# Ordering the opening and the convolution of an S4 + gated-MLP kernel by a list of units

## The chip, the cores and the metric

The kernel runs on one core of a Trainium2 chip. A core has five engines that run their own instruction streams in order and wait for each other through semaphores: PE (TensorE, matmuls; its weight loads are shown apart as PEld), DVE (VectorE), ACT (ScalarE), POOL (GpSimd) and SP (SyncE, which here only issues DMAs). SP, ACT and POOL can each issue DMAs from a queue of their own. The metric is the device time of one execution in microseconds (us). Two times of one kernel are compared by runs of both on the same chip.

## What is computed

The input x has 2048 rows of 576 channels. One modulation vector c gives six rows of 576 through `w_mod`. The first block is a normalised, modulated long convolution; its kernel K (576 channels, 2048 taps) comes from 128 complex poles per channel. The second is a gated MLP. Cut to what matters:

```python
mod = (silu(c) @ w_mod)                     # sa, ca, ga, sb, cb, gb
h = layernorm(x) * (1 + ca) + sa
logdA = dt * (A_re + 1j*A_im);  dB = dt * (B_re + 1j*B_im)
P = exp(logdA[:, :, None] * arange(L))      # 576 x 128 x 2048, complex
K = einsum("dn,dnl,dn->dl", C, P, dB).real
y = irfft(rfft(h) * rfft(K))[:L] + h * Dskip # causal convolution
x = x + ga * y
h = layernorm(x) * (1 + cb) + sb
z = gelu(h @ w_in);  z1, z2 = halves of z
g = w_sp @ layernorm(z2) + b_sp
x = x + gb * ((z1 * g) @ w_out)
```

## The kernel before

**Stages.** `ssm` does the modulation, the first norm, the convolution kernel and the convolution; `Mlp.phase_a` and `phase_b` do the gated MLP, some 1350 us of the span, and are not touched. All of the change is in `ssm`, in what I call the opening (to the first ticks of the loop) and the convolution loop.

**Poles.** `poles(c0, c1, ...)` is a generator: it issues the loads of the seven pole arrays on SP, and each `next` of it then emits a further piece of elementwise work on DVE and ACT. `split3` splits a result into three bf16 parts and writes them to DRAM (`pa_d`, `pb_d`) from POOL's queue. `p0` handles the first chunk of channels (tiles 144 wide, kept in one tile named `et`), `p1` the other three at once (432 wide, tiles `t_n_...`). `poles_load(c)` brings a chunk's parts back as matmul operands `lb`, `lc`, `la`.

**Kernel units.** The kernel's 36 groups of 16 channels each pass through: `e_unit` (three matmuls of `lb` with the table `sel`, then two exponentials on ACT, 1024 and 512 wide, into `et`), `t_unit` (phase matmuls of `lc`, `la` with `sel`, rounding on DVE, or by an ACT pass `ft<-ps` and DVE from group 10 on), `s_unit` (cosine and sine on ACT), `p_unit` (products on DVE into `pg`, `et`), `kg_unit` (32 small matmuls, a copy `kab`), `d_unit` (Dskip), `k1_unit` (matmuls, copy into the `k1` tile of eight groups). Exponential and sine need different ACT tables; each change of table is one ACT_TABLE_LOAD.

**Modulation and norm.** `mod_load(k)` loads one of the six weight blocks in two halves (tiles `wm`, or borrowed `k` tiles for k = 0, 1); `mod_unit(k)` multiplies it by silu(c) and spreads the row over the partitions. The rows 2, 1, 0 give `gar`, `cga`, `sga`/`gsp`, which the first norm needs; 3, 4, 5 are for the MLP. `ln_load(i)` loads four of the 16 row blocks of x into one of two tiles `ln_x`; `ln_stats(i)` computes their mean and deviation; `ln_rows(b)` scales block b on DVE; `ln_pair(b)` does blocks b and b+1: matmuls against the first Fourier stage, in two halves of 288 channels, each copied to `st1o` by ACT and written to `u1_d` in DRAM from POOL's queue.

**Convolution units.** `u_load`/`u_unit` bring back and transform the input, `z_unit` multiplies it by the kernel's transform, `v_unit` goes back one stage and writes `v_d`, `y_load`/`y_unit` the last stage. `u_load` reads rows of all 16 blocks, so it needs every `ln_pair`.

**What sets the order.** The program is written unit by unit. A framework then orders instructions on each engine by a cost model of its own; those issued through `mlp.tied.<engine>` are kept in program order among themselves (they all show line 152, the helper's line, in the profile). V and T (DVE and PE) are `tied` at first and become free later. After a written opening, a loop over 40 ticks runs `p_unit` of tick-2, `t_unit` of tick, `s_unit` of tick-1, `kg_unit` and `d_unit` of tick-3, `k1_unit` of tick-4 and every third tick three `e_unit`s, in one fixed order below tick 10 and another from it. In ticks 0 to 7 the loop also holds one whole `ln_pair`, and the rest of p1 and of the modulation.

Of the kernel before, what the change touches and what calls it, by code (L numbers as in the profile page):

```python
# [9 lines left out]
F32 = mybir.dt.float32  # L10
# [3 lines left out]
AF = mybir.ActivationFunctionType  # L14
# [150 lines left out]
def ssm(tc, I, x1_d, consts_s, dram, mod_d, mlp):  # L165
    nc = tc.nc
    V, A, G, T, S = nc.vector, nc.scalar, nc.gpsimd, nc.tensor, nc.sync
    magic, halfpi, one = consts_s[:, 0:1], consts_s[:, 1:2], consts_s[:, 2:3]
    HC = 288
    CW = 16 * 9 * 128  # L170
    with ExitStack() as ctx:
# [3 lines left out]
        early = ctx.enter_context(ExitStack())  # L175

        u1_d = dram.tile([4, 16, 2, 32, D], F32, name="u1_d")
# [4 lines left out]
        def ps2():  # L182
            return psp.tile([128, 2, 512], F32, name="ps")
# [5 lines left out]
        small = cp.tile([128, 6, 128], F32, name="small")  # L189
# [3 lines left out]
        tb = tabs.enter_context(tc.tile_pool(name="tb", reuse_waits="tile", bufs=2))  # L193
# [141 lines left out]

        gar = ep.tile([128, D], F32, name="gar", bufs=1)
        cga = ep.tile([128, D], F32, name="cga", bufs=1)
# [37 lines left out]
        x4s = {}  # L375
        r1t = {}

        def ln_load(i):
            x4s[i] = ep.tile([128, 4, D], F32, name="ln_x")
            S.dma_start(x4s[i], I["x"][:, 4 * i:4 * i + 4])  # L380

        def r1_load(i):
            r1t[i] = ep.tile([128, 2, 2, 32], F32, name="r1t"), ep.tile([128, 2, 2, 32], BF, name="cs")
            S.dma_start(r1t[i][0], I["c_r1t"][:, 2 * i:2 * i + 2])
            S.dma_start(r1t[i][1], I["c_cs"][:, 2 * i:2 * i + 2])

        lns = {}

# [25 lines left out]
        def ln_rows(b):  # L414
            i, j = divmod(b, 4)
            nm, r = lns[i]
            n = x4s[i][:, j]
            V.scalar_tensor_tensor(n, n, nm[:, j:j + 1], cga, op0=ALU.add, op1=ALU.mult)
            rt = ep.tile([128, 64], F32, name="rt", bufs=4)
            V.tensor_scalar(rt, r1t[b // 2][0][:, b % 2].rearrange("p r k -> p (r k)"), r[:, j:j + 1], None, op0=ALU.mult)  # L420
            return n, rt, r1t[b // 2][1][:, b % 2].rearrange("p r k -> p (r k)")

        def ln_pair(b):
            pair = [ln_rows(b), ln_rows(b + 1)]
            for h in range(2):
                c = slice(HC * h, HC * h + HC)
                o = ep.tile([128, 4, HC], F32, name="st1o")
                pms = [ps2(), ps2()]
                for t, (n, rt, cs) in enumerate(pair):
                    for x, y, st in ((cs, gsp, True), (rt, n, False)):  # L430
                        for g in range(4):
                            rows = slice(32 * g, 32 * g + 32)
                            T.matmul(pms[g // 2][64 * t:64 * t + 64, g % 2, :HC], x[rows], y[rows, c], start=st, stop=not st, skip_group_check=True)
                for k, pm in enumerate(pms):
                    A.activation(o[:, 2 * k:2 * k + 2], pm[:, :, :HC], AF.Copy)
                G.dma_start(u1_d[:, b:b + 2, :, :, c].rearrange("g b r k d -> (b r k) g d"), o)


        k1t = {}
# [229 lines left out]
                at(ty, y_load, c, r)  # L669
                at(ty + 1, y_unit, c, r)  # L670

        p0 = poles(0, 1, mlp.tied.gpsimd, tb.tile([128, 1536], F32, name="et", bufs=5))
        S.dma_start(cT, I["c"])
        mod_load(2)
        ln_load(0)
        S.dma_start(sel, I["c_sel"])
        mod_load(1)
        S.dma_start(small, I["c_small"][:, 128:].rearrange("p (i c) -> p i c", i=6))
        p1 = poles(1, 4, mlp.tied.gpsimd)
        mod_load(0)  # L680
        r1_load(0)
        ln_load(1)
        S.dma_start(msk, I["c_msk"])
        S.dma_start(dsk, I["dsk"])
        r1_load(1)
        V, T = mlp.tied.vector, mlp.tied.tensor
        for _ in range(3):
            next(p0)
        mod_init()
        for _ in p0:  # L690
            pass
# [7 lines left out]
        next(p1)  # L699
        V = nc.vector  # L700
        ln_stats(1)
        sb = cs = None
        for tick in range(NG + 4):
            if tick == 9:
                early.close()
                cs = ctx.enter_context(tc.tile_pool(name="cs", reuse_waits="tile", bufs=1, side="right"))
                sb = ctx.enter_context(tc.tile_pool(name="sb", reuse_waits="tile", bufs=2, side="right"))
                wpre = ctx.enter_context(tc.tile_pool(name="wpre", reuse_waits="tile", bufs=2, side="right"))
            if 9 <= tick < 13:
# [12 lines left out]

            def lag(fn, n):
                if 0 <= tick - n < NG:
                    fn(tick - n)

            if tick == 0:
                for g in range(3):
                    e_unit(g)
            go(y_load)  # L730
            go(u_load)
            es = iter(range(tick, tick + 3) if tick % 3 == 0 and 0 < tick < NG else ())

            def e_one():
                for g in es:
                    e_unit(g)
                    break

            if tick < 10:
                go(z_unit)  # L740
                lag(p_unit, 2)
                lag(t_unit, 0)
                lag(s_unit, 1)
                go(v_unit)
                lag(kg_unit, 3)
                go(u_unit)
                lag(k1_unit, 4)
                go(y_unit)
                lag(d_unit, 3)
                if tick == 0:  # L750
                    T = nc.tensor
                for _ in range(3):
                    e_one()
            else:
                go(z_unit)
                lag(p_unit, 2)
                lag(t_unit, 0)
                lag(s_unit, 1)
                lag(kg_unit, 3)
                lag(k1_unit, 4)  # L760
                go(y_unit)
                go(v_unit)
                e_one()
                go(u_unit)
                lag(d_unit, 3)
                e_one()
                e_one()
            if tick < 5:
                next(p1, None)
                next(p1, None)  # L770
            if tick == 0:
                mod_load(3)
            if 3 <= tick < 6:
                mod_unit(tick)
                if tick < 5:
                    mod_load(tick + 1)
            j = tick
            if j < 8:
                if j in (2, 4):
                    ln_stats(j // 2 + 1)  # L780
                ln_pair(2 * j)
                if j < 6:
                    r1_load(j + 2)
                if j in (1, 3):
                    ln_load(j // 2 + 2)
            if tick in (3, 13, 21):
                poles_load(1 + tick // 10, mlp.tied.gpsimd)


        tabs.close()  # L790
        mlp.nc = mlp.tied
# [1428 lines left out]
```

## Time and profile before

| what | us |
|---|---|
| median of three runs (lowest to highest) | 1770.71 (1767.39 to 1773.47) |
| the profiled execution's own time | 1773.18 |
| its span, first to last instruction | 1771.4 |
| busy in the span: PE, DVE, ACT, POOL | 1666.3, 1259.8, 831.7, 244.1 |
| span up to the end of the convolution stage (about) | 420 |

The profile is one execution. A row of a timeline gives start, duration, engine, line, operation, tiles and count; in square brackets stand the idle time of the engine just before it and what ended that. A row of the DMA list gives the tiles, the issuing queue, the count, the size of one and the median us from issue to landing. Busy time on PE is modelled from pipelined matmuls and is not PE at its peak.

### The profile page before, as it was taken

Reading aid. Unit: us, or ns where it says so; the run is one execution under the profiler, and the core shown is the slowest. Engines: PE = TensorE matmul, PEld = TensorE weight load, DVE = VectorE, ACT = ScalarE, POOL = GpSimd, SP = SyncE. Lnnn points to the kernel's source line nnn. Section 1 sums busy time; section 2 is a strip of 40 time slices with the busy share of each in tenths; the row PEclk is TensorE's granted clock in tenths of the full one; section 3 lists DMA queues with packets and bytes.
Section 4 is the critical chain, followed back from the end, with each engine's and each line's share of the span. In section 5 each row is a group of like instructions: output and inputs, shape, how many; then the busy total and the mean of one; then the engine's idle time right before and its main releaser. Section 6 shows DMA issues by size and latency. Waiting matters only on the chain.

```text
span 1771.4 us, 36409 instructions
## 1 busy us (share of the span) xinstructions
PE 1666.3 (94%) x15174; PEld 1244.5 (70%) x15174; DVE 1259.8 (71%) x2259; ACT 831.7 (47%) x1118; POOL 244.1 (14%) x400
## 2 busy tenths in 40 slices
PE   3687999997899999999999999999999999999999
PEld 1244555565455445787878888888888888888887
DVE  6876999866998997788898767788334477334432
ACT  4758998844577666455434443333232223122210
POOL 3331232233122211000000000000111100111100
PEclk9578999998999999999999999999999999999999
DMA  9466545689598889777665886773766573556531
GB/s 253 139 198 216 162 124 168 198 231 306 179 281 254 244 234 265 267 276 246 222 214 175 306 299 236 255 248 124 251 226 223 195 229 98 195 203 216 188 112 41
DMA packets 183381, 376.24 MB, mean 212 GB/s; under 512 B 39360, under 2 KB 103488, under 8 KB 182448
## 3 DMA queue, kind: packets, MB, share of 16 engines
q1 hardware_dynamic: 140416, 175.23, 32.8%
q0 software_dynamic: 36896, 172.01, 29.6%
q10 hardware_dynamic: 5904, 26.67, 3.7%
q8 instruction: 119, 1.95, 0.5%
q14 instruction: 46, 0.38, 0.1%
HBM read 263.11 MB, written 101.31 MB: 206 GB/s over the span
## 4 chain that ended last, share of the span: by engine, by line
PE 62%; DVE 16%; issue 7%; DMA 6%; ACT 5%; POOL 2%; SPq 1%; ACTq 0%; POOLq 0%; DVEq 0%
PE ps L152 54%; DVE bsz L152 2%; DVE n L152 1%; PE pk L530 1%; DVE zset L152 1%; PE pk L513 1%; DVE gt L152 1%; DVE rq L152 1%; DMA ln_x<-in_x 1%; DMA zset<-set_d 1%; PE pk L592 1%; DVE wso L152 1%; DMA wst<-in_w_in 1%; DMA k<-in_w_mod 1%; PE pk L600 1%
## 5 line engine op out<-in xcount | busy, mean ns | idle before, releaser
L152 PEld LDWEIGHTS <-zset 128*128 128x128 f16 x7182 | 701.9, 98 | 93.0 <-DVE zset L152 8.9
L152 PE MATMUL ps<-wsp,zset 128*128 128x256 f16 x6048 | 667.5, 273 | 7.7 <-DVE zset L152 6.9
L152 PE MATMUL pz<-wz,nt 128*128 128x512 f16 (+1 forms) x1120 | 223.8, 360 | 10.4 <-ACT nt L152 3.8
L152 ACT ACTIVATE z<-gt 128x1024 f16<-128x1024 f32 x56 | 59.0, 1054 | 287.7 <-DVE gt L152 287.7
L152 PEld LDWEIGHTS <-nt 128*128 128x128 f16 x1120 | 109.5, 99 | 118.7 <-issue 5.4
L152 DVE SCALAR_TENSOR_TENSOR gt<-ps,sc,bsp 128x512 f32<-128x512 f32 x36 | 27.0, 750 | 204.7 <-PE ps L152 203.0
L1928 POOL DMA_DIRECT2D zset<-set_d x96 | 50.8, 529 | 869.6 <-PE ps L152 614.3
L152 PE MATMUL ps<-wout,z 128*128 128x288 f16 x1344 | 170.0, 286 | 0.0
L152 PEld LDWEIGHTS <-z 128*128 128x128 f16 x1344 | 131.5, 98 | 33.0
L152 PE MATMUL ps<-n2o,zset 128*128 128x256 f16 x1134 | 128.2, 273 | 0.0
L152 DVE TENSOR_TENSOR raw<-raw 128x512 f32<-128x512 f32 (+2 forms) x228 | 119.1, 528 | 12.1 <-DMA raw<-z_d 7.8
L152 DVE SCALAR_TENSOR_TENSOR gt<-ps,sc,gt 128x512 f32<-128x512 f32 (+1 forms) x180 | 122.2, 696 | 7.6
L152 DVE TENSOR_TENSOR zset<-raw,zset 128x1792 f16<-128x1792 f32 x48 | 96.9, 2019 | 16.4 <-ACT zset L152 16.4
L152 ACT ACTIVATE zset<-raw 128x1792 f16<-128x1792 f32 x48 | 81.0, 1691 | 56.8 <-PE ps L152 23.1
L152 DVE TENSOR_TENSOR z<-ps,z 128x512 f32<-128x512 f32 (+1 forms) x126 | 72.0, 599 | 36.8 <-ACT z L152 25.0
L152 ACT ACTIVATE wsp<-raw,sc 128x1792 f16<-128x1792 f32 x25 | 44.6, 1784 | 42.7 <-DVE raw L152 35.0
L152 ACT ACTIVATE z<-z,sc 128x1024 f32<-128x1024 f32 x21 | 24.1, 1148 | 75.9 <-DVE z L152 71.9
L152 ACT ACTIVATE z<-pz,sc 128x512 f32<-128x512 f32 (+1 forms) x96 | 51.8, 581 | 14.1 <-DMA z_d<-z 7.9
L152 ACT ACTIVATE z<-z,nm,r 128x1152 f32<-128x1152 f32 x24 | 31.5, 1342 | 52.6 <-DVE nm L152 31.9
L152 PE MATMUL ps<-n2q,wf 128*128 128x512 f16 x252 | 55.7, 379 | 0.0
L152 PE MATMUL ps<-wout,z1b 128*128 128x288 f16 x384 | 52.6, 286 | 0.5 <-ACT z1b L152 0.5
L501 DVE TENSOR_TENSOR pg<-et,ft 128x1024 f32<-128x1024 f32 x36 | 43.8, 1217 | 11.5 <-ACT ft L489 11.4
(357 smaller groups left out, 2462.6 us busy)
## 6 DMA issues: line engine op xcount, KB each, us to landing
zset<-set_d POOLq DMA_DIRECT2D x96, 896.0 KB, 5.0
raw<-z_d SPq DMA_DIRECT2D x48, 512.0 KB, 5.6
set_d<-zset ACTq DMA_DIRECT2D x24, 896.0 KB, 6.0
z_d<-z POOLq DMA_DIRECT2D x32, 576.0 KB, 9.7
zset<-wa_d POOLq DMA_DIRECT2D x18, 896.0 KB, 4.9
raw<-in_w_spT SPq DMA_DIRECT2D x25, 512.0 KB, 4.3
set_d<-zset SPq DMA_DIRECT2D x12, 896.0 KB, 5.5
u_d<-st1o POOLq DMA_DIRECT2D x16, 576.0 KB, 4.6
```

The source lines that it names most:

```text
L152: return self.tc.keep_in_program_order(f(*a, **k))
L501: V.tensor_tensor(pr, pi, c3[:, :, None, :].to_broadcast([128, 16, 2, 32]), op=ALU.mult)
L513: T.matmul(pm[32 * j:32 * j + 32, 64 * i:64 * i + 64], x_[:, c], y_[:, c].rearrange("p s j -> p (s j)"), start=st, stop=not st, skip_group ...
L530: T.matmul(pm[64 * ri:64 * ri + 64, 128 * i:128 * i + 128], kk[:, i], r1[ri], start=True, stop=True, skip_group_check=True)
L592: T.matmul(pm[:, w * j:w * j + w], cst[k // 8][:, k % 8], k1t[c][:, k, :w], start=True, stop=True)
L600: T.matmul(pm, inva, zz[:, 0], start=True, stop=False)
L1928: self.nc.gpsimd.dma_start(o, self.set_d[f, j - 1] if j else self.wa_d[f])
```

## The change

The written opening and the ticks 0 to 8 of the loop become one string of tokens, which `early_steps` walks: a letter names the unit, a digit its group, a trailing `g` or `a` puts a load on GpSimd's or ACT's queue instead of SP's. `0` and `#` start p0 and p1, `O` and `P` are one `next` of them, `Q` is `poles_load`, `w` `mod_load`, `M` `mod_unit`, `x` `ln_load`, `S` `ln_stats`, `R` the two `ln_rows` of a pair, `A` and `B` the two halves of `ln_pair` (now `ln_half`), `V` and `T` free the engine. From tick 9 on, three strings give the order of the units by tick modulo 3; exponent groups are drawn singly, two in one tick, one in the next, none in the third. No unit's arithmetic changes.

```diff
-        def mod_load(k):
+        def mod_load(k, q):
...
-                S.dma_start(wmt[k][hh], I["w_mod"][:, k, hh])
+                q.dma_start(wmt[k][hh], I["w_mod"][:, k, hh])
...
-        def ln_pair(b):
-            pair = [ln_rows(b), ln_rows(b + 1)]
-            for h in range(2):
...
+        def ln_half(b, pair, h):
...
-        poles_load(0, mlp.tied.gpsimd)
-        mod_unit(2)
-        ln_stats(0)
-        next(p1)
-        next(p1)
-        mod_unit(1)
-        mod_unit(0)
...
-            if tick < 10:
-                go(z_unit)
-                lag(p_unit, 2)
-                lag(t_unit, 0)
-                lag(s_unit, 1)
-                go(v_unit)
-                lag(kg_unit, 3)
...
-                ln_pair(2 * j)
...
+        early_steps("0 m O O O T c r0g O O r1g l I x0 w2g O O O O M2 O # b a O Q0 e0 V w1g e1 P P t0 P e2 w0g s0 x1g S0 "
+                 "t1 P P s1 p0 M1 M0 P S1 P t2 t3 k0 P s2 p1 R0 A0 B0 e3 R1 e4 r2 d0 w3 e5 s3 k1 p2 A1 B1 t4 x2g R2 P "
...
+        exps = iter(range(9, NG))
+        lagged = {"t": (t_unit, 0), "s": (s_unit, 1), "p": (p_unit, 2), "k": (kg_unit, 3), "d": (d_unit, 3), "1": (k1_unit, 4)}
+        passed = {"z": z_unit, "v": v_unit, "u": u_unit, "y": y_unit}
+        for tick in range(9, NG + 4):
...
+            for n in ('kpt1svyzdeeu', 'ktespy1dzvu', 'ktvsdzuyp1')[tick % 3]:
+                if n == "e":
+                    for g in exps:
+                        e_unit(g)
+                        break
...
```

Three places of the built programs show what moves. The first is the start of PE's stream; `ps<-...,ec` is a modulation product (`wm` is block 2, the two `k_` tiles blocks 1 and 0), `lb` an exponent's operand. Before:

```order
L152 MATMUL ps<-wm,ec 32x288 x12
L152 MATMUL ps<-mpart,small 128x288 x2
L152 MATMUL ps<-k_122,ec 32x288 x12
L152 MATMUL ps<-mpart,small 128x288 x2
L152 MATMUL ps<-k_140,ec 32x288 x12
L152 MATMUL ps<-mpart,small 128x288 x2
L152 LDWEIGHTS lb
L152 MATMUL ps<-sel,lb 128x512
```

and of the change:

```order
L349 MATMUL ps<-wm,ec 32x288 x12
L354 MATMUL ps<-mpart,small 128x288 x2
L448 LDWEIGHTS lb
L448 MATMUL ps<-sel,lb 128x512
...
L349 MATMUL ps<-k_276,ec 32x288 x12
L354 MATMUL ps<-mpart,small 128x288 x2
L349 MATMUL ps<-k_340,ec 32x288 x12
```

The products of blocks 1 and 0 moved behind the first three exponent units and the phase units 0 and 1, which stand at the line of dots.

The second is POOL's stream, which holds its DMA issues. Before:

```order
L152 DMA pb_d<-pt 64x3x144 x2
L152 DMA pa_d<-pt 64x3x144 x4
L152 DMA pb_d<-pt 64x3x144 x2
L152 DMA pa_d<-pt 64x3x144 x2
L152 MEMSET lb 32x1152
L152 DMA lb<-pb_d 48x1152 x2
L152 DMA lc<-pa_d 48x1152 x2
L152 DMA la<-pa_d 48x1152 x2
```

and of the change:

```order
L152 DMA wm<-in_w_mod 96x1728 x2
L152 DMA pa_d<-pt 64x3x144 x2
L152 DMA pb_d<-pt 64x3x144 x2
L152 DMA pa_d<-pt 64x3x144 x2
L152 MEMSET lb 32x1152
L152 DMA lb<-pb_d 48x1152 x2
L152 DMA lc<-pa_d 48x1152 x2
L152 DMA la<-pa_d 48x1152 x2
L152 DMA k_276<-in_w_mod 96x1728 x2
L152 DMA k_340<-in_w_mod 96x1728 x2
L152 DMA ln_x<-in_x 128x2304
```

Block 2 of the weights came in between the pole writes, blocks 1 and 0 and the second x block behind the operands of the first exponents; all four were on SP's queue.

The third is DVE's stream within the poles of the first chunk (144 wide), after its logarithm. Before:

```order
L152 TENSOR_TENSOR t_sq_212<-t_tau_160,pt 128x144
L152 TENSOR_TENSOR t_sq_214<-t_lw,pt 128x144
L152 TENSOR_TENSOR pt<-t_sq_212,pt 128x144
L152 TENSOR_TENSOR pt<-t_sq_214,pt 128x144
L152 TENSOR_SCALAR t_ph<-t_ph 128x144
L152 TENSOR_TENSOR et<-et 128x144
```

and of the change:

```order
L152 TENSOR_TENSOR t_sq_188<-t_tau_120,pt 128x144
L238 TENSOR_TENSOR t_n_A_im<-t_dt,t_n_A_im 128x432
L152 TENSOR_TENSOR t_sq_190<-t_lw,pt 128x144
L152 TENSOR_TENSOR pt<-t_sq_188,pt 128x144
L239 TENSOR_SCALAR t_n_A_im<-t_n_A_im 128x432
L243 TENSOR_TENSOR t_n_A_re<-t_dt,t_n_A_re 128x432
L152 TENSOR_TENSOR pt<-t_sq_190,pt 128x144
L152 TENSOR_SCALAR t_ph<-t_ph 128x144
L152 TENSOR_TENSOR et<-et 128x144
L240 TENSOR_SCALAR t_n_A_im<-t_n_A_im 128x432
L152 TENSOR_SCALAR et<-t_ph 128x144
L247 TENSOR_TENSOR t_q_289<-t_n_C_im,t_n_B_im 128x432
```

The 432-wide steps of the other poles, which stood behind all of the first chunk's, now stand between its steps, the one that reads `t_n_B_im` among them.

More of the change, by code (lines that the diff above doesn't have):

```diff
@@ L421, in ln_rows @@
             return n, rt, r1t[b // 2][1][:, b % 2].rearrange("p r k -> p (r k)")
-        def ln_pair(b):
-            pair = [ln_rows(b), ln_rows(b + 1)]
-            for h in range(2):
[L426 to L436, printed above, removed]
+        def ln_half(b, pair, h):
+            c = slice(HC * h, HC * h + HC)
+            o = ep.tile([128, 4, HC], F32, name="st1o")
+            pms = [ps2(), ps2()]
+            for t, (n, rt, cs) in enumerate(pair):
+                for x, y, st in ((cs, gsp, True), (rt, n, False)):
+                    for g in range(4):
+                        rows = slice(32 * g, 32 * g + 32)
+                        T.matmul(pms[g // 2][64 * t:64 * t + 64, g % 2, :HC], x[rows], y[rows, c], start=st, stop=not st, skip_group_check=True)
+            for k, pm in enumerate(pms):
+                A.activation(o[:, 2 * k:2 * k + 2], pm[:, :, :HC], AF.Copy)
+            G.dma_start(u1_d[:, b:b + 2, :, :, c].rearrange("g b r k d -> (b r k) g d"), o)
         k1t = {}
@@ L670, in ssm @@
                 at(ty + 1, y_unit, c, r)
[L672 to L684, printed above, removed]
@@ L685, in ssm @@
-        r1_load(1)
-        V, T = mlp.tied.vector, mlp.tied.tensor
[L687 to L691, printed above, removed]
-        poles_load(0, mlp.tied.gpsimd)
-        mod_unit(2)
-        ln_stats(0)
-        next(p1)
-        next(p1)
-        mod_unit(1)
-        mod_unit(0)
[L699 to L709, printed above, removed]
+        p1 = p0 = None
@@ L725, in lag @@
                     fn(tick - n)
-            if tick == 0:
-                for g in range(3):
-                    e_unit(g)
             go(y_load)
             go(u_load)
[L732 to L737, printed above, removed]
-            if tick < 10:
-                go(z_unit)
-                lag(p_unit, 2)
-                lag(t_unit, 0)
-                lag(s_unit, 1)
-                go(v_unit)
-                lag(kg_unit, 3)
[L746 to L780, printed above, removed]
-                ln_pair(2 * j)
[L782 to L786, printed above, removed]
+            for n in ('kpt1svyzdeeu', 'ktespy1dzvu', 'ktvsdzuyp1')[tick % 3]:
[3 more added lines that the diff above has]
+                        break
+                elif n in lagged:
+                    lag(*lagged[n])
+                else:
+                    go(passed[n])
+            if tick in (13, 21):
                 poles_load(1 + tick // 10, mlp.tied.gpsimd)
```

65 lines of the change are left out of this document (60 added, 5 removed), and 2 rows, old and new, of the table T.

## The prediction

> **What bounds the kernel now.** The first view read is the busy time by stage. I cut the span where the program changes character: at the first exponential (47.67 us), at the first phase unit of the steady loop (168.78 us), where the last exponentials begin (342.48 us), and at the start of the gated MLP (420 us). Columns: span; busy us of PE, PE weight loads, DVE, ACT, POOL; granted TensorE clock, DMA share, GB/s.
>
> ```profile
> 0.00:47.67 47.67, 19.94 (x87) 7.51 (x87) 27.42 (x91) 21.39 (x45) 17.96 (x33) 1.00 0.97 252
> 47.67:168.78 121.11, 93.62 (x1252) 47.08 (x1251) 91.84 (x192) 88.89 (x133) 29.67 (x45) 0.70 0.56 171
> 168.78:342.48 173.70, 159.32 (x2400) 100.02 (x2400) 160.18 (x200) 159.32 (x213) 49.12 (x85) 0.99 0.58 168
> 342.48:420.00 77.52, 74.95 (x764) 48.79 (x764) 47.86 (x71) 43.51 (x61) 28.96 (x49) 1.00 0.90 255
> 420.00:1771.40 1351.40, 1318.47 (x10676) 1041.14 (x10676) 932.50 (x1708) 518.62 (x670) 118.40 (x190) 0.99 0.66 218
> ```
>
> The change reaches the first four rows; the fifth follows the fourth and only shifts. The lead (first row) is full of DMA (0.97). In the loop (third row) PE, DVE and ACT are all 92% busy: little is left. In the middle (second row) none is above some 77%, though it does the same kinds of unit. That is the room: 121.11 us in which DVE works 91.84. At the loop's 92% the same work would take 100 us.
>
> The second view is the timeline of the lead, engine by engine.
>
> ```profile
> 8.13 0.43 SPq L231 DMA_DIRECT2D t_n_log_dt<-in_A_log_dt  x1
> 15.98 5.58 SPq L231 DMA_DIRECT2D t_n_C_re<-in_A_C_re  x1
> 25.28 0.69 SPq L231 DMA_DIRECT2D t_n_B_im<-in_A_B_im  x1
> 20.13 0.31 DVE L152 TENSOR_TENSOR pt<-t_sq,pt 128x144 bf16<-128x144 f32 x1 [0.39 <-ACT pt L220]
> 34.02 0.61 DVE L152 TENSOR_TENSOR t_q<-t_n_C_im,t_n_B_im 128x432 f32<-128x432 f32 x1 [2.64 <-DMA t_n_B_im<-in_A_B_im]
> 25.38 1.03 POOL L152 DMA_DIRECT2D lb<-pb_d  x2 [1.90 <-DMA pb_d<-pt]
> lb<-pb_d POOLq DMA_DIRECT2D x2, 108.0 KB, 6.6
> la<-pa_d POOLq DMA_DIRECT2D x2, 108.0 KB, 12.2
> 41.85 2.14 PE L152 MATMUL ps<-k,ec 96*32 96x288 f32 x12 [1.34 <-DMA k<-in_w_mod]
> 44.80 2.29 PE L152 MATMUL ps<-mpart,small 128*128 128x288 f32 x4 [0.81 <-ACT mpart L351]
> 47.67 1.02 ACT L451 ACTIVATE et<-ps 128x1024 f32<-128x1024 f32 x1 [2.93 <-PE ps L152]
> ```
>
> The first poles end on DVE at 20.4; their operand lb is fetched at 25.38 and lands 6.6 us later, at 32 to 33. But the exponent's matmul is pinned on PE behind the modulation products, whose last weights come at 41.85, so it runs at 47.0: some 14 us of waiting that it has no need of. The other poles (432 wide) wait too: their last input, B_im, is put to use at 34.02, after SP's queue had stood 5.58 us on one issue.
>
> **The lead, costed.** The sizes of what the queues carry:
>
> ```profile
> k<-in_w_mod SPq DMA_DIRECT2D x4, 648.0 KB, 14.8
> ln_x<-in_x SPq DMA_DIRECT2D x4, 1152.0 KB, 9.4
> sel<-in_c_sel SPq DMA_DIRECT2D x1, 518.0 KB, 12.1
> small<-in_c_small SPq DMA_DIRECT2D x1, 384.0 KB, 17.7
> t_n_B_im<-in_A_B_im SPq DMA_DIRECT2D x1, 216.0 KB, 8.7
> et<-in_A_B_im SPq DMA_DIRECT2D x1, 72.0 KB, 2.2
> 54.98 2.85 DVE L152 RECIPROCAL t_rnd<-t_n_B_re 128x432 f32<-128x432 f32 x1
> ```
>
> Now SP carries ahead of the last pole input: the first chunk 0.50 MB (seven of 72 KB), small 0.38, sel 0.52, x 1.15, the poles 1.51 (seven of 216); sum 4.1 MB, where it carried two modulation weights of 1.30 MB (two halves each) more. GpSimd adds w2 (1.30 MB) beside it. At the row's 252 GB/s, 4.1 MB take 16 us and 5.4 MB 21 us; with the first microseconds, in which little moves, I take B_im at 23 us, 10 us earlier than 33.4.
>
> This has a price. DVE's order now puts large pole instructions between those of the first chunk, the product that reads B_im among them, and DVE runs in order. So the first chunk no longer ends at 20.4: after 23 us some 12 small steps at 0.31 us, ten large at about 0.5 and two round trips to ACT remain, about 10 us, end 33. Then pa_d goes out (two issues, 1.25), lb is cleared (1.05) and fetched. In before, lb and la took 6.6 and 12.2 us in a full DMA stage; now the queues are nearly empty at 35 us (w3 alone runs before it), and I take 4. First exponential near 40 to 41 instead of 47.67: **7 us** gained. Bounds: 0 (B_im as late as before, p0's end at 43) to 12 (no wait in p0's steps).
>
> w1, w0 and the second x block follow la on GpSimd, issued near 39 us: 2.59 MB at 252 GB/s is 10.3 us, so M0's product runs at 50 to 52 instead of 41.85 to 47. The norm's first matmul needs it through sga and gsp:
>
> ```profile
> 55.91 0.47 PE L433 MATMUL ps<-gsp,cs 32*64 32x288 bf16 x4 [0.74 <-ACT et L451]
> 154.92 0.47 PE L433 MATMUL ps<-gsp,cs 32*64 32x288 bf16 x6 [0.77 <-ACT st1o L435]
> 57.76 1.22 DVE L479 COPY ft<-ps 128x1024 f32<-128x1024 f32 x1
> 108.05 1.82 SPq L380 DMA_DIRECT2D ln_x<-in_x  x1
> 116.44 1.18 DVE L408 BATCH_NORM_STATS2 bs<-ln_x 128x6 f32<-128x288 f32 x3 [4.85 <-DMA ln_x<-in_x]
> 128.83 1.15 ACT L489 ACTIVATE ft<-ft,consts_s 128x1024 f32<-128x1024 f32 x1 [6.42 <-DVE ft L484]
> 146.63 1.23 DVE L501 TENSOR_TENSOR pg<-et,ft 128x1024 f32<-128x1024 f32 x1 [5.80 <-ACT ft L489]
> 168.78 1.17 ACT L482 ACTIVATE ft<-ps,consts_s 128x1024 f32<-128x1024 f32 x1
> L489 ACT ACT_TABLE_LOAD x13 | 16.7, 1283 | 0.2
> ```
>
> M0's product to the first norm matmul took 14 us (41.85 to 55.91), so that matmul comes at 64 to 66, 8 to 10 later. I cost this at nothing, because poles, phases and products of units 0 and 1 now fill DVE there (its first phase copy, at 57.76 before, can start near 49, when the poles' remaining steps after 33 are done: twenty at 0.5, the reciprocal of 2.85 and some 14 tiny ones, 16 us). If that cover is gone it costs those 8 to 10 us: the slower rival below.
>
> **The middle, costed.** The same units run in both, but for ACT's table loads: 35 in the program against 32, 3 x 1.283 = 3.8 us more. Two stalls of DVE before show what the list changes. The fourth x block waited for its buffer, was issued at 108.05, and DVE stood 4.85 us on it at 116.44, with ACT standing 6.42 behind. Its stats stood one DVE group after the pair that freed the buffer; they now stand some 27 DVE rows behind it, about 13 us of work by the durations above against the 8.4 us that the load took. And the three exponents of a group ran as one block on ACT with the sine waiting behind; DVE stood 5.80 for that at 146.63. They are now spread singly. These sum to 10.65 us of DVE idle (the ACT wait overlaps the first).
>
> DVE idles 29.27 us in the middle. Its work there is now 91.84 less the 3.5 us of pole steps done earlier, 88.3. Nothing better than before: 76%, 116 us. Like the loop: 92%, 96 us. The named stalls removed and the rest kept: 29.3 - 10.65 = 18.6 us idle, and 88.3 + 18.6 = 107 us. Of the distance from 116 I give back 3.8 for the table loads, as ACT is nearly as busy as DVE: 110.7. So the middle ends at 40.7 + 110.7 = 151.4 instead of 168.78: **17.4 us** gained, of it 7 from the lead.
>
> **The loop.** Its three ticks now have three unlike orders of units. What a period leaves:
>
> ```profile
> 296.15:319.41 23.26, 21.55 (x320) 13.47 (x319) 21.06 (x29) 21.01 (x29) 6.38 (x11) 1.00 0.56 167
> 319.41:342.48 23.07, 22.27 (x336) 14.35 (x335) 21.71 (x28) 20.63 (x28) 6.13 (x10) 1.00 0.62 177
> 341.86 0.60 ACT L602 ACTIVATE v<-pk 128x512 f32<-128x512 f32 x1 [1.66 <-issue]
> ```
>
> PE leaves 0.8 to 1.7 us of 23. At most 1.7 x 7.5 periods = 13 us come of it; an order that costs ACT a second wait like the 1.66 us would lose as much. v still stands just ahead of the exponents' table load, so that wait stays. I take 0.2 us a period, **1.5 us** gained, bounds -9 to +9. The tail is PE-bound (74.95 of 77.52) with the same matmuls: nothing.
>
> Sum: 17.4 + 1.5 = 19 us. The profiled execution took 1773.18 (span 1771.4), which gives 1754; it is 2.5 above the runs' median of 1770.71, from which it is **1752**.
>
> **Two rules weighed.** GpSimd issued four pole writes in 2.48 us while DVE had much waiting, and six in 3.75 while DVE was 10.00 of 10 us busy: 0.62 us each in both.
>
> ```profile
> 14.15 2.48 POOL L152 DMA_DIRECT2D pa_d<-pt  x4
> 73.91 3.75 POOL L152 DMA_DIRECT2D pa_d<-pt  x6 [4.12 <-DVE pt L222]
> 70.00:80.00 10.00, 7.02 (x70) 2.73 (x65) 10.00 (x21) 5.95 (x10) 6.09 (x10) 0.50 0.52 133
> ```
>
> The Trainium skill (SBUF — State Buffer, "A bandwidth-pool intuition that's wrong") warns that some DVE copies lock GpSimd out of writing descriptors, so that its DMAs starve; that speaks against moving weights there. By it each weight issue would wait for one large DVE step, 4 x 0.7 = 3 us on M0; the rows show none of it, and by them the sum keeps zero.
>
> **The rivals.** (1) *The late norm decides: slower.* Pairs start 8 to 10 us later behind the weights on GpSimd's queue, and the loop cannot start before the last pair is written and read back. It decides if the 16 halves still need the 99 us from 55.91 to 154.92: then 65 + 99 + 14 = 178, 9 us late, **1780**. Against it: the pairs' matmuls and copies are far less than 99 us; they waited for others.
>
> (2) *No lead.* B_im lands as late as before: p0 ends later and the exponents gain nothing; the spread halves give a little. Gain 0 to 5: **1768**.
>
> (3) *The middle keeps its 76%.* 40.7 + 116 + 3.8 = 160.5, 8 us: **1762**, and a loop that loses 0.3 us a period makes it 1765.
>
> (4) *The middle runs as the loop does.* 40.7 + 96 = 137, 32 us gained, **1737**. For it the clock must rise: the middle's row has 0.70, and 93.62 us of PE at the loop's 92% are 102 us, gain 26. The Trainium skill (TensorE: Matmul & The Clock Gate, "HAM oscillation") says that idle gaps above about 3.4 us halve the clock and steady work restores it. By that rule a denser middle frees PE and 1737 stands; by an unchanged clock it is 1745.
>
> That the change does not do what it says is excluded for the exponents (PE's order shows them ahead), not for the loop.
>
> **How the numbers follow.** Forecast (gain 10 to 28) 0.50; (4) 0.15; (3) 0.10; these are faster, 0.75. (2) 0.10, mostly no change. (1) 0.15, slower. About 0.3% (5.3 us) is what a measurement here can tell from no change. The likeliest is 1752, its own range 1743 to 1761. The range for 8 in 10 takes in (2), (3) and most of (4): 1736 to 1774, leaving 0.06 below and 0.14 above.
>
> **What would show it.** First exponential on ACT at 38 to 43; B_im's product on DVE near 23; the first norm matmul at 62 to 68; no wait over 2 us of the norm's stats for x; the first magic phase on ACT near 151; loop periods of 22.5 to 23.3; granted clock of the middle above 0.70. Wrong if the exponent starts after 46, if pairs end last before the loop, or if a period exceeds 24.

## The result and the profile after

The changed kernel takes 1753.33 us (median of 5 runs, 1750.43 to 1755.88) beside 1770.89 us for the kernel before on the same chip: 0.9909 of before, 95% interval 0.9889 to 0.9928. A second comparison, on the chip of the experiments below, gave 0.9929 (0.9902 to 0.9957). The forecast of 1752 is 0.9894 of the 1770.71 that it started from: inside the first interval, just below the second. Two of its terms were wrong and cancelled each other.

The first view is the busy time by stage of the changed kernel, cut at the same events as before (first large exponential, first phase pass on ACT, last exponent group, and about the start of the MLP, 400 here and 420 there):

```profile
0.00:40.53 40.53, 9.41 (x35) 3.40 (x36) 29.18 (x96) 25.06 (x49) 18.45 (x35) 1.00 0.85 226
40.53:157.09 116.56, 92.89 (x1289) 48.62 (x1288) 87.70 (x187) 87.15 (x131) 35.73 (x54) 0.82 0.61 183
157.09:322.67 165.58, 158.10 (x2401) 98.28 (x2401) 157.01 (x198) 159.72 (x214) 49.17 (x85) 0.98 0.66 188
322.67:400.00 77.33, 76.31 (x777) 49.07 (x773) 48.66 (x72) 42.39 (x58) 27.80 (x48) 1.00 0.90 252
400.00:1749.50 1349.50, 1317.65 (x10678) 1041.73 (x10678) 933.54 (x1709) 520.03 (x673) 119.35 (x191) 0.99 0.66 219
```

The lead is 7.1 us shorter (47.67 to 40.53). The middle is only 4.6 shorter (121.11 to 116.56), and DVE is still busy for 75% of it. The loop, which was to change little, is 8.1 shorter (173.70 to 165.58). The tail is nearly as it was (to the MLP mark used below it is 1.0 us longer).

The second view, timelines of the changed kernel, holds the rows that the prediction named:

```profile
21.92 0.61 DVE L247 TENSOR_TENSOR t_q<-t_n_C_im,t_n_B_im 128x432 f32<-128x432 f32 x1 [1.59 <-DMA t_n_B_im<-in_A_B_im]
37.37 1.28 ACT L152 ACT_TABLE_LOAD   x1
39.24 1.28 ACT L449 ACT_TABLE_LOAD   x1
40.53 1.02 ACT L449 ACTIVATE et<-ps 128x1024 f32<-128x1024 f32 x1
63.35 0.31 PE L431 MATMUL ps<-gsp,cs 32*64 32x288 bf16 x2 [0.25 <-ACT gsp L365]
94.56 1.18 DVE L408 BATCH_NORM_STATS2 bs<-ln_x 128x6 f32<-128x288 f32 x3 [4.22 <-DMA ln_x<-in_x]
120.14 1.18 DVE L408 BATCH_NORM_STATS2 bs<-ln_x 128x6 f32<-128x288 f32 x3 [2.61 <-DMA ln_x<-in_x]
134.47 1.19 ACT L433 ACTIVATE st1o<-ps 128x576 f32<-128x576 f32 x2 [2.65 <-DMA u_d<-st1o]
135.17 0.39 PE L469 MATMUL ps<-sel 48*128 48x512 bf16 x2 [2.37 <-ACT st1o L433]
136.63 1.23 DVE L477 COPY ft<-ps 128x1024 f32<-128x1024 f32 x1 [3.98 <-PE ps L465]
157.09 1.15 ACT L480 ACTIVATE ft<-ps,consts_s 128x1024 f32<-128x1024 f32 x1
```

The reader is to see three things. B_im, the first exponential and the first norm matmul come where they were forecast. DVE still waits for blocks of x, now twice (4.22 and 2.61). And at 134.47 begins a chain of waits that the kernel before did not have there: a copy of a norm half waits for its buffer `st1o` to be written out, PE for that copy, DVE for PE.

### The profile page after: what moved, and what is told of

Read it like the earlier page. It is cut to its first block, busy times and chain, and to the rows that moved or that the text cites. A ratio compares the mean times of both kernels' runs of the same rounds, so it can differ in the third digit from the quotient of the medians.

```text
span 1749.5 us, 36390 instructions
## 1 busy us (share of the span) xinstructions
PE 1654.4 (95%) x15174; PEld 1241.1 (71%) x15174; DVE 1256.1 (72%) x2259; ACT 834.3 (48%) x1121; POOL 250.5 (14%) x412
## 4 chain that ended last, share of the span: by engine, by line
PE 32%; issue 28%; DVE 18%; DMA 4%; POOL 3%; ACT 2%; SPq 0%; POOLq 0%; ACTq 0%; DVEq 0%
PE ps L152 28%; POOL zset L1906 2%; DMA zset<-set_d 2%; DVE bsz L152 2%; DVE zset L152 1%; DVE n L152 1%; DVE gt L152 1%; DVE rq L152 1%; DVE wsp L152 1%; PE pk L578 1%; PE pk L598 1%; PE pk L590 1%; DVE pg L499 1%; DVE wso L152 1%; DVE ft L481 1%
## 5 line engine op out<-in xcount | busy, mean ns | idle before, releaser
L152 DVE SCALAR_TENSOR_TENSOR wsp<-raw,sc,wsp 128x1792 f16<-128x1792 f32 x25 | 51.9, 2078 | 0.0
```

Source lines behind the costliest of these rows:

```text
L152: return self.tc.keep_in_program_order(f(*a, **k))
```

## The experiments

Ratios are to the kernel before, timed on the same chip. The other columns are the first large exponential, the first phase pass on ACT (where the loop begins; the expectations call it the first magic phase) and `sc<-ones` on ACT, the MLP's first scale, from one profile each; the MLP mark stands for the end of all that was changed.

| run | ratio (95% interval) | exponential | phase pass | MLP mark | span |
|---|---|---|---|---|---|
| before | 1 | 47.67 | 168.78 | 425.70 | 1771.4 |
| the change | 0.9909 (0.9889, 0.9928) | 40.53 | 157.09 | 406.92 | 1749.5 |
| after_again | 0.9929 (0.9902, 0.9957) | 39.66 | 158.38 | 407.96 | 1752.9 |
| open_new_loop_old | 0.9971 (0.9956, 0.9987) | 39.38 | 160.75 | 417.38 | 1768.0 |
| open_old_loop_new | 0.9964 (0.9952, 0.9977) | 45.59 | 167.49 | 415.48 | 1763.7 |
| loop_old_exps_single | 1.0035 (1.0016, 1.0053) | 37.93 | 153.79 | 425.41 | 1774.5 |
| loop_new_exps_block | 0.9981 (0.9970, 0.9992) | 39.43 | 156.99 | 414.87 | 1765.0 |
| st1o_three | 0.9896 (0.9870, 0.9921) | 39.32 | 150.46 | 399.96 | 1746.4 |
| st1o_two_ctl | 0.9903 (0.9890, 0.9915) | 40.22 | 157.47 | 406.58 | 1750.2 |
| halves_together | 0.9921 (0.9908, 0.9934) | 38.54 | 156.57 | 405.36 | 1749.7 |
| mod_first | 0.9951 (0.9933, 0.9969) | 53.95 | 166.22 | 416.86 | 1763.9 |
| w_sp | 0.9986 (0.9970, 1.0002) | 42.90 | 168.00 | 416.29 | 1766.3 |
| w2_sp | 0.9979 (0.9962, 0.9996) | 38.99 | 172.19 | 420.23 | 1763.2 |
| w10_sp | 0.9984 (0.9973, 0.9995) | 49.19 | 169.99 | 418.01 | 1766.7 |

Kernels with the same opening show how far a mark scatters from profile to profile: the first exponential stands at 37.93 to 40.53 in five profiles with the opening of the change, and at 45.59 and 47.67 with that of before.

### Opening and loop apart

The opening of the change with the loop of before:

```diff
-            for n in ('kpt1svyzdeeu', 'ktespy1dzvu', 'ktvsdzuyp1')[tick % 3]:
+            for n in ('zptsvku1ydeee' if tick == 9 else 'zptsk1yveudee' if tick % 3 == 0 else 'zptsk1yvud'):
```

> The opening of the change, with the loop's unit order from before (tick 9 and the later ticks as they were, exponents in blocks of three). Theory A (the two parts add: opening 11 us, loop 9 us, as the markers of the two traces suggest): about 1760 us, loop periods (from one exponent group's table load to the next) 22.4 to 23.3 us as before, start of the third group's table load near 194. Theory B (the prediction's split: opening 17, loop 1.5): about 1754, with the loop as fast as in the change. Theory C (the loop runs faster in the change because the opening leaves it less behind, not by its own order): about 1753, periods of 20.3 to 22.4 us.

The loop of the change behind the opening of before:

```diff
+            if tick >= 9:
+                for n in ('kpt1svyzdeeu', 'ktespy1dzvu', 'ktvsdzuyp1')[tick % 3]:
...
-            if tick < 10:
+            elif tick < 9:
```

> The opening of before (ticks 0 to 8 as they were), with the loop's three unit orders of the change and exponents drawn singly. Theory A: the loop alone brings about 9 us, 1762 us, with periods of 20.3 to 22.4 us. Theory B: it brings 1.5 us, 1769. Theory C: it brings nothing, 1770 to 1772, with periods of 21.9 to 23.3 as before.

At the MLP mark the opening alone stands 8.3 us ahead of before (425.70 - 417.38), the loop alone 10.2, the change 18.8: the two add, as theory A has it. The table loads ahead of the exponents show it period by period: with the old loop the periods from the third on are 22.39, 21.93, 23.26, 23.06, 23.26, 23.07, those of before within 0.01; with the new loop behind the old opening 21.09, 20.29, 21.64, 21.70, 22.42, 20.94, those of the change within 0.1. A period's length belongs to the loop's order alone, and theory C falls. So does B: the loop was worth 10, not 1.5.

The times show less than the marks: 0.9971 is 5 us, 0.9964 is 6. The repeat of the change was for that:

> The change itself, beside runs of other versions on one chip. The opening alone gave 0.9971 and the loop alone 0.9964 of before, though at the end of the convolution stage their traces stood 8.3 and 10.2 us ahead and the change 18.8. Theory A (the parts add, and what is missing from each alone is jitter of the waits for weight loads in the gated MLP): the change measures 0.990 to 0.994 here, and its profile has its last marker before the MLP within 0.5 us of the one before (406.9). Theory J (the first comparison flattered the change): 0.994 or above.

It gave 0.9929 and a mark 1.0 us behind the first (0.5 had been allowed). A gain of 12 us there agrees with the sum of the parts, 5 + 6. What lies between mark and end is told under the hardware, below.

### What in the loop does it

Exponents spread, other units in the old order; and the reverse:

```diff
-            for n in ('kpt1svyzdeeu', 'ktespy1dzvu', 'ktvsdzuyp1')[tick % 3]:
+            for n in ('zptsk1yveude', 'zptsk1yveud', 'zptsk1yvud')[tick % 3]:
```

> The change with one thing taken back: in the loop the units other than the exponents stand in the order of before in every tick, the exponents stay single (two, one, none). Theory D (the loop's gain comes from spreading the exponents, so that ACT's block of three no longer holds up the sines): as the change, 1753, periods of 20.3 to 22.4 us. Theory E (the gain comes from the order of the other units, the kernel matmuls and their copy ahead of the new phases): about 1762, periods of 22 to 23.3.

```diff
-            for n in ('kpt1svyzdeeu', 'ktespy1dzvu', 'ktvsdzuyp1')[tick % 3]:
+            for n in ('kpt1svyzdeeeu', 'ktspy1dzvu', 'ktvsdzuyp1')[tick % 3]:
```

> The change with one thing taken back: in the loop the three exponents of a group are drawn in one block in the first of three ticks, all other units stay in the order of the change. Theory D (spreading the exponents is the gain): about 1762, periods of 22 to 23.3 us. Theory E (the order of the other units is the gain): as the change, 1753, periods of 20.3 to 22.4 us. If both this and the run with the old order lie half-way, near 1757, the two parts share it.

Neither theory holds by itself. The new order with a block of three takes 158.11 us for seven periods, where before takes 159.36 and the change 150.65: the order alone gives 1.2. The old order with single exponents is 8 us slower at the mark than the old order with a block (425.41 to 417.38). The groups of ACT's table loads say why; the change first, then the old order with single exponents:

```profile
L487 ACT ACT_TABLE_LOAD x14 | 18.0, 1283 | 0.2
L449 ACT ACT_TABLE_LOAD x11 | 14.1, 1283 | 0.2
```

```profile
L487 ACT ACT_TABLE_LOAD x23 | 29.5, 1283 | 0.4
L449 ACT ACT_TABLE_LOAD x21 | 26.9, 1283 | 0.4
```

In the old order the sines of the next tick come ahead of its exponent, so each spread exponent swaps tables there and back. The new strings put two exponents at the end of one tick (`...deeu`) and the third ahead of the sines of the next (`kte s...`): spread, and still one pair of loads in a period. The order of units is worth little by itself, but it makes the spreading free.

Where DVE's idle time went shows in its groups in the stretch 183 to 322 us: before, and the new loop behind the old opening. The last column is idle time ahead of the group, with its cause.

```profile
L483 DVE SCALAR_TENSOR_TENSOR ft<-ft,ps 128x1024 f32<-128x1024 f32 x19 | 23.0, 1213 | 4.7 <-ACT ft L482 4.7
L535 DVE COPY k<-pk 128x512 f32<-128x512 f32 x8 | 5.5, 683 | 2.1 <-PE pk L530 2.1
```

```profile
L483 DVE SCALAR_TENSOR_TENSOR ft<-ft,ps 128x1024 f32<-128x1024 f32 x19 | 23.1, 1218 | 0.8 <-ACT ft L482 0.6
L535 DVE COPY k<-pk 128x512 f32<-128x512 f32 x9 | 6.2, 688 | 0.1
```

DVE had stood for ACT's phase pass, which was queued behind the block of exponents, and for the kernel matmuls on PE. Little of both waits is left. In one period of before the table load comes at 296.15 on ACT, three exponents follow, the phase pass starts at 302.08, and DVE waits for it:

```profile
303.29 1.22 DVE L483 SCALAR_TENSOR_TENSOR ft<-ft,ps 128x1024 f32<-128x1024 f32 x1 [1.62 <-ACT ft L482]
```

Over seven periods DVE is idle for 11.8 of 159.36 us in before and for 5.6 of 150.65 us in the change. That is 6.2 of the 8.7 us; the rest is time in which DVE counts as busy, 147.6 against 145.1 us, and is not explained.

### The middle's missing six microseconds

The waits at 134 suggest the two buffers of `st1o`. A third one needs space; `mpart` and `sga` were laid into tiles that are free at that time:

```diff
-        sga = ep.tile([128, D], F32, name="sga", bufs=1)
...
-            mpart = ep.tile([128, D], F32, name="mpart", bufs=1)
+            if k == 2:
+                mpart = cga
+            elif k < 2:
+                mpart, sga = sp[1], sp[0]
+            else:
+                mpart = ep.tile([128, D], F32, name="gar", bufs=1)
...
-            o = ep.tile([128, 4, HC], F32, name="st1o")
+            o = ep.tile([128, 4, HC], F32, name="st1o", bufs=3)
```

> The change, with a third buffer for the copied halves of the norm (st1o); the space comes from mpart and sga, which are laid into tiles that are free then. Theory F (at 131 to 135 us ACT waits 2.65 us for a half to be written out, PE stands 2.37 us behind it, its clock drops to half from 135 to 152, and that is the part of the middle that was not won): the clock stays at 0.9 or more up to 152, the first magic phase comes on ACT 4 to 6 us earlier, at 151 to 153, and the time is about 1748 us. Rival G (the halves wait for PE, ACT and the norm's rows as well, and one buffer more only moves the wait): first magic at 156 to 158, time as the change, 1753.

The control has the same edit but leaves `st1o` at two buffers:

> The control to the third buffer: mpart and sga laid into the same other tiles, but st1o with two buffers as in the change; the order of instructions on every engine is that of the version with three. Theory F (the third buffer is what won 7 us there): ACT's wait for the write-out near 131 to 135 and the halved clock up to about 150 are back, first magic at 156 to 159, time as the change (0.993 of before). Rival P (the new places of mpart and sga won it): first magic at 150 to 152, 0.990.

Stretches of the change, of three buffers, and of the control (span; busy PE, PE weight loads, DVE, ACT, POOL; granted clock; DMA):

```profile
135.00:150.00 15.00, 14.03 (x146) 6.83 (x151) 8.79 (x10) 8.34 (x13) 2.55 (x4) 0.52 0.43 152
```

```profile
130.00:150.00 20.00, 14.95 (x307) 8.42 (x304) 14.30 (x24) 15.17 (x22) 4.53 (x6) 1.00 0.66 228
39.32:150.46 111.14, 85.98 (x1291) 46.01 (x1290) 87.24 (x186) 87.15 (x131) 35.69 (x54) 0.89 0.63 191
```

```profile
40.22:157.47 117.25, 92.23 (x1291) 48.83 (x1290) 87.37 (x186) 87.15 (x131) 35.67 (x54) 0.87 0.60 180
136.85 1.19 ACT L439 ACTIVATE st1o<-ps 128x576 f32<-128x576 f32 x2 [2.23 <-DMA u_d<-st1o]
```

With a third buffer the wait is gone, the clock is 1.00 there, the middle takes 111.1 us instead of 116.6, and the phase pass comes at 150.46. The control has the wait again and nearly the marks of the change (157.47, 406.58), as theory F has it. But its 7.0 us behind the version with three buffers do not all come from the buffer, as the copy `kab` shows, the last of its kind on ACT ahead of the wait:

| run | first exponential | copy `kab` | phase pass | from `kab` to the phase pass |
|---|---|---|---|---|
| st1o_three | 39.32 | 127.65 | 150.46 | 22.8 |
| st1o_two_ctl | 40.22 | 131.88 | 157.47 | 25.6 |
| the change | 40.53 | 129.03 | 157.09 | 28.1 |
| after_again | 39.66 | 130.19 | 158.38 | 28.2 |

So the wait and what follows it cost 5.3 us in the change and 2.8 in the control. The other 4.2 us of the control arise ahead of that wait: 0.9 at the first exponential, and about 3 more up to 57 us, where its modulation products took twice as long on PE. The control first, then three buffers:

```profile
51.13 2.29 PE L360 MATMUL ps<-k,small 128*128 128x288 f32 x4 [0.75 <-ACT k L357]
```

```profile
50.19 1.24 PE L360 MATMUL ps<-k,small 128*128 128x288 f32 x4 [0.75 <-ACT k L357]
```

This varies from run to run: the change has 1.24 us for that product and after_again, the same kernel, 2.29. That the buffer causes the wait is shown; what it is worth lies between 2.8 and 5.3 us. In the change PE is 94% busy from 135 to 150 but at half clock, and stays so until 152; in the control the clock is back at 1.00 from 146. The longer half clock goes with the larger loss, but no run sets the clock apart from the wait.

The whole times do not settle it. The control's 0.9903 is what rival P had forecast (0.990), not F (0.993), and is 1.2 us from the 0.9896 of three buffers, with overlapping intervals; the 0.9929 of after_again is 5.8 us from it. No version here is shown to be faster than the change; three buffers are the best candidate.

Spreading the halves was tested directly, with every `B` token moved right behind its `A`:

```diff
-... R1 e4 r2 d0 w3 e5 s3 k1 p2 A1 B1 t4 x2g R2 P A2 Q1 B2 p3 ... A4 M5 d3 B4 r6 k4 A5 R6 B5 ...
+... R1 e4 r2 d0 w3 e5 s3 k1 p2 A1 B1 t4 x2g R2 P A2 B2 Q1 p3 ... A4 B4 M5 d3 r6 k4 A5 B5 R6 ...
```

> The change with the second half of each norm pair put right behind the first one in the list, so that the halves are no longer spread. Theory M (spreading them is worth what two buffers let it be: a second half waits for the write-out of the one before it but one, 4.8 us): longer waits of ACT for u_d writes, first magic 3 to 6 us later than in the change (157 to 158), 0.995 to 0.997 of before. Rival N (the middle is set by its sum of work): first magic within 1.5 us of the change, 0.992 to 0.994.

Rival N holds: 0.9921, and the mark 1.6 us ahead of the change's. That the halves are spread brings nothing that these runs can see.

### The lead: order and queue

```diff
-O Q0 e0 V w1g e1 P P t0 P e2 w0g s0 x1g S0 t1 P P s1 p0 M1 M0 P S1 ...
+O Q0 w1g w0g x1g M1 M0 e0 V e1 P P t0 P e2 s0 S0 t1 P P s1 p0 P S1 ...
```

> The change with the modulation products of blocks 1 and 0 put ahead of the first exponents and their weights and the second block of x issued at once behind the exponents' operands. Theory K (the prediction: the exponents' lead is what is won in the opening, and the norm is covered): first large exponential near 47, first norm matmul near 56 instead of 63, the middle ends 5 to 7 us later, time about 1759. Rival L (in the middle the norm's halves end last, so an earlier norm makes up for later exponents): first magic phase at 157 or before, time 1753 or below.

0.9951, slower as K has it: the large exponential comes at 53.95 (K had 47), the phase pass 8 to 9 us late. But the norm's first matmul did not come earlier (63.07, where K had 56). The weights landed late: PE waited for them, 4.71 us up to 39.88 and 0.38 up to 42.39, and block 0's product ran at 47.49, 5 us ahead of the change. `gsp` was then ready at 59.95 (63.29 in the change), and the norm's first matmul stood on PE behind the phase matmuls of units 0 and 1. How much of the delay is the exponents and how much the re-ordering behind them, one run does not tell.

The loads were put back on SP's queue, all (`w2g`, `w1g`, `w0g`, `x1g` without the `g`), then in two parts:

> The change with modulation weights 2, 1 and 0 and the second block of x back on SP's queue, at the same places of the list. Theory H (the queue matters: weights 2 stand ahead of the pole inputs on SP, 1.3 MB or 5 us, and delay the first chunk's poles, which stand behind the large steps on DVE): B_im's product on DVE near 27 instead of 21.9, first exponential near 45 instead of 40.5, time about 1757; in its favour the waits of about 2 us before each of GpSimd's pole writes from 42 to 53 go away, worth at most 1 or 2. Theory I (all of it is covered): every mark within 1 us of the change, 1753.

> Of the run with all weights on SP only the first part: weights 2 back on SP's queue ahead of the pole inputs, the rest as in the change. There B_im's product came at 31.2 and the stage ended 8 to 9 us late (time 1767). Theory Q (SP's queue ahead of the pole inputs does it): B_im near 30, and 5 to 9 us of the loss, 0.996 to 0.998 of before. Rival R (it is the weights 1 and 0 that stand ahead of la's loads in the DMA engines): B_im at 26 or earlier, first exponential within 2 us of the change, 0.993 to 0.995.

> The other part: weights 1 and 0 and the second block of x back on SP's queue, weights 2 stay on GpSimd's. Theory Q: B_im near 20, SP issues the 2.6 MB at once behind the pole inputs, first exponential within 2 us of the change, the waits of 2 us before GpSimd's pole writes gone: 0.991 to 0.994 of before. Rival R (the weights delay the writes of the first chunk's poles and the loads of lb, lc, la behind them): la's load waits for pa_d's write some 4 us, first phase copy on DVE at 48 to 51 instead of 43, 0.996 to 0.998.

Each takes most of the gain away (0.9979 to 0.9986). In w_sp B_im's product came at 31.22 and the exponential at 42.90 (27 and 45 in H), but the time is 1767 where H had 1757: most of the loss lies in the middle, which H had not costed. For weights 1 and 0 the rows show the path: the change first, then w10_sp (DMA list and timeline).

```profile
wm<-in_w_mod POOLq DMA_DIRECT2D x2, 648.0 KB, 9.0
```

```profile
wm<-in_w_mod POOLq DMA_DIRECT2D x2, 648.0 KB, 16.4
37.96 0.56 ACT L218 ACTIVATE pt<-t_n_A_re 128x432 bf16<-128x432 f32 x1 [11.80 <-DMA pb_d<-pt]
39.31 0.52 POOL L152 DMA_DIRECT2D lb<-pb_d  x1 [10.05 <-DMA pb_d<-pt]
49.19 1.02 ACT L449 ACTIVATE et<-ps 128x1024 f32<-128x1024 f32 x1 [1.14 <-PE ps L448]
```

SP issues the 2.6 MB of weights at once behind the pole inputs, at 15.15. Block 2's weights on GpSimd's queue then take 16.4 us instead of 9.0, the small pole writes behind them in that queue land at 38 to 39, and `lb` cannot be fetched before. Rival R holds in kind: it is `lb` that waits, 10 us for `pb_d`, where a wait of 4 us of `la` was expected, and the first exponential is 8.7 late. In w2_sp B_im's product does come late (28.77, as Q has it), but the first exponential does not: 38.99, for DVE then ends the first chunk's poles (last step at 25.85) ahead of that product, where in the change they end at 29.08, between the large steps. The phase pass still comes at 172.19. Why it loses 15 us in the middle is open: the framework sorted that opening anew, PE waited 3.50, 2.63 and 5.08 us between 64 and 76, and its clock was at half from 70 to 80 and from 150 to 170.

## Why the prediction came out right, and where it was wrong

**The lead: right in size, in part by luck.** 7 us were forecast and 7.1 came (a mark that scatters by 2.6 us between profiles), with B_im at 21.9 (forecast 23; before it stood at 34.02, not at 33.4 as the forecast wrote) and the first norm matmul at 63.35 (64 to 66). What carries it is what the forecast read first, that the exponents stand ahead of the modulation products on PE (mod_first), and that little is ahead of the pole writes in the DMA engines (w10_sp). Two terms behind it were off and cancelled. The first chunk's last step ran at 29.08, not at 33, and `lb` landed in 2.9 us (4), so that its matmul ran on PE at 35.41 and not near 39. The last wait was ACT's order instead, which the forecast had at nothing: a step of the other poles needs a buffer `pt` that the first chunk's last write to `pa_d` must free, and more pole steps and two table loads (37.37 and 39.24) stand between it and the exponential at 40.53.

```profile
35.19 0.56 ACT L218 ACTIVATE pt<-t_n_A_im 128x432 bf16<-128x432 f32 x1 [2.18 <-DMA pa_d<-pt]
```

So the first chunk's end does bear on the exponential, but by way of that write and not of `lb`. That an early B_im is needed for it is not shown: in w2_sp B_im came 7 us later and the exponential no later, though there the first chunk does not wait for B_im.

**The weights' queue.** The forecast let a late M0 cost nothing because DVE is covered. Nothing contradicts it, but no run moves M0 alone: mod_first brought M0's product only 5 us forward. The rule of the Trainium skill weighed there (SBUF — State Buffer, "A bandwidth-pool intuition that's wrong") is not seen here either: single pole writes still took 0.62 to 0.63 us. What GpSimd does pay is its own queue: four of the other poles' writes stood 1.85 to 2.01 us each behind the weights, 42 to 50 us; neither DVE nor ACT shows a wait for them there.

```profile
42.32 0.63 POOL L152 DMA_DIRECT2D pb_d<-pt  x1 [1.88 <-DMA k<-in_w_mod]
47.57 0.63 POOL L152 DMA_DIRECT2D pb_d<-pt  x1 [2.00 <-DMA k<-in_w_mod]
```

**The middle: mis-sized, 110.7 forecast, 116.6 measured.** The step that failed is "the named stalls removed and the rest kept". The sine behind the exponents (5.80) did go; of the wait for x 2.61 was left, and 4.22 came anew for the third block, against the forecast that no such wait would pass 2 us. And the rest was not kept: three pairs of copies of halves now come within 7 us (127.95, 130.14, 134.47 on ACT), two buffers are too few for them, and the clock halved behind that wait. With a third buffer the middle takes 111.1 us. The 3.8 us given back for three more table loads stood in the wrong stage: the middle has ten loads before and after, and the lead has seven where it had four. Without them the forecast of the middle was 106.9 and the miss 9.7 us. The rival "the middle keeps its 76%" came true for the middle (75%), not for the time.

**The loop: mis-sized, 1.5 forecast, 9 to 11 measured** (eight periods take 179.15 us before, 169.92 in the change, 168.12 in open_old_loop_new), at the bound of 9 and beyond it. The step that failed is "I take 0.2 us a period", argued from PE's 0.8 to 1.7 us of idle time a period and from one wait of ACT. The largest waits that went were DVE's for the phase pass behind the block of exponents: 0.66 to 3.95 us in five of the eight periods. The prediction had named a wait of that kind in the middle (5.80, for the sine) and not looked for it in the loop. The forecast range of periods, 22.5 to 23.3, was left at the lower end: of the eight in the change one took 22.5, the others 19.3 to 22.4.

**The sum.** 17.4 + 1.5 was forecast, 18.8 us stood at the MLP mark. The phase pass came 11.7 us earlier instead of 17.4, 5.7 less; from it to the mark the change takes 249.8 us where before took 256.9, 7.1 gained instead of 1.5, 5.6 more. That the two misses meet within 0.1 us is luck. (The 7.1 are less than the periods' 9, since the tail from the last exponents to the mark is 1.0 longer, 83.2 to 84.2, and the third exponent of the first group now stands behind that phase pass.) The late norm did not decide: its last half was copied at 151.05, before at 156.48. Of the two times of rival (4), 1737 contains the loop's 1.5 us and 1745 does not; nothing rests on it.

## What to carry to other kernels

When a list of units is re-ordered, look for the same wait in every stage before costing one of them: the block of exponents was priced in the middle and overlooked in the loop, where it came back in most periods. Work that needs another ACT table can be spread without further table loads if all its pieces fall between the last sine of one round and the first of the next. And when stalls are taken out of a stage, count the buffers of what then runs closer together, since the next wait stands there.

## What the runs showed of the hardware

**A wait of some 2 us can halve PE's clock.** In the change PE stood 2.37 us, and the granted clock went from 1.00 to 0.64 in the 1.8 us after 135.2 and to 0.50 until 152; in the control it was 0.54 from 139 to 141, behind a wait of 1.96 that ended at 137.56, and 1.00 again from 146. With three buffers the longest wait near there was 1.61 and the clock stayed at 1.00. One wait's length does not decide alone: behind 2.26 us of waiting that ended at 75.41 in the change the clock was still 1.00, and it fell in the next wait, of 2.89 us, at 77.5. The Trainium skill (TensorE: Matmul & The Clock Gate, "HAM oscillation — how this bites in real kernels") puts the limit at about 3.4 us of idle time; these runs show less than that to be enough. By the same page ("What's actually happening") some 3.4 us of steady work restore the clock, while here PE was 94% busy for 15 us at half clock. Why it stayed low is open.

**A granted clock of 1.00 did not always mean fast matmuls.** The control's view gives 1.00 from 50 to 56 us, where its four matmuls `ps<-k,small` took 2.29 us; the same four took 1.24 us in st1o_three at 50.19, also at 1.00. The duration of equal matmuls has to be read beside that column.

**One queue's bulk slows another's.** The 9.0 and 16.4 us of the same 648 KB loads on GpSimd's queue, without and with 2.6 MB on SP's, agree with the Trainium skill (DMA: Bandwidth & Descriptors, "Queues, rings and completion order"), by which each DMA engine takes turns between the queues that have work.

**The MLP does not pass gains on exactly.** From the mark to the end the profiles take 1342.6 (the change) to 1350.6 us (open_new_loop_old), though ACT and DVE run the same list there. That profile is the slowest of its kernel's twelve runs, 6.0 us above their median, and the change's lies 2.1 below its own, so a difference of spans overstates the one of medians. The difference arises in the first 300 us, where ACT waits for weights from DRAM:

```profile
522.99 1.06 ACT L152 ACTIVATE wsst<-wsst 128x1024 f32<-128x1024 f32 x1 [6.68 <-DMA wsst<-in_w_spT]
531.09 8.36 PE L152 MATMUL pz<-wz,nt 128*128 128x512 f16 x28 [4.56 <-ACT nt L152]
```

These rows are of open_new_loop_old, 106 and 114 us behind its mark; the change has no wait of PE over 1 us from 60 to 125 us behind its own. Whether such waits depend on when the MLP begins, or only on the run, was not tried.
